# Loading each weight piece as two transfers of 64 partitions, and moving two transposes by one product

## The chip, the cores and the metric

The kernel runs on one NeuronCore of a Trainium2 chip. The metric is the device time of one execution in microseconds. All runs of the kernel before lie between 2293 and 2320 us. A ratio is the mean time of one kernel's runs over the mean of the other's runs of the same rounds on the same chip, so it is not quite the ratio of the medians that stand beside it.

## The reference

Two branches on `x` (2048 tokens of 1024) are mixed by a gate. Branch A is a recurrent attention with memory, in 64 segments of 32 tokens. Each segment needs the 8 memory rows that the segment before produced, so the 64 steps cannot overlap freely. Branch B is a gated feed-forward network.

```python
for s in range(n_seg):                      # 64 segments, one after the other
    xs = x[:, s * seg_len:(s + 1) * seg_len, :].copy()
    h = jnp.concatenate([mem, xs], axis=1)  # 8 + 32 rows
    q = jnp.einsum('btd,dhe->bhte', h, Wq)  # Wq, Wk, Wv: 1024 x 32 heads x 128
    k = jnp.einsum('btd,dhe->bhte', h, Wk)
    v = jnp.einsum('btd,dhe->bhte', h, Wv)
    scores = jnp.einsum('bhqe,bhke->bhqk', q, k) * scale
    # ... mask, softmax -> p ...
    o = jnp.einsum('bhqk,bhke->bhqe', p, v)
    o = jnp.einsum('bhte,hed->btd', o, Wo)
    mem = o[:, :M, :].copy()
    outs.append(o[:, M:, :])
# branch B: gelu(x @ w_gate) * (x @ w_up) @ w_down;  result g * a + (1 - g) * b
```

## The kernel before

The four weight matrices of branch A are cut into 64 pieces of 512 KB (128 partitions by 2048 bf16). The program does not hold all of them on the chip at once. It has 52 slots, and 12 of them are shared by two pieces each: when a product has used one piece, its slot is refilled with the other. So every step fetches 12 pieces, in the order in which slots come free: 2 of Wk, 2 of Wq, 5 of Wv, 3 of Wo. The order of products alternates from step to step, so that each fetch serves two uses.

```python
        PAIRS = {"k": (0, 2), "q": (0, 2), "v": (0, 1, 2, 4, 6), "o": (0, 2, 4)}
        ORDER = (("k", 0), ("q", 0), ("v", 0), ("k", 1), ("q", 1), ("o", 0), ("v", 1), ("o", 1))
        # ... (cut)
        def fetch(n):
            k, t = uses[n][done[n]], slots[n]
            if paired(k):
                lane = f"sl{n}"
            else:
                lane = f"res{nlane[0] % 8}"
                nlane[0] += 1
            op("sp", lambda e: e.dma_start(dst(t, k), src(k)), wr=[t.r()], lane=lane)
        # ... (cut)
        def spent(k):                    # called behind each product
            n = home[k]
            done[n] += 1
            if done[n] < len(uses[n]) and uses[n][done[n]] != k:
                fetch(n)
```

`op` records an instruction and finds its waits from the regions that it reads and writes; a lane is a semaphore, and the program counts a load as 16 on it (in the trace, 16 packets of 4 bytes a piece). SyncE ("sp") issues all these loads in order. A row of a Wk, Wq or Wv piece is 4 KB in one run; a row of a Wo piece is two runs of 2 KB, one for each of its two heads. In the trace they are packets of 4,096 and 2,048 bytes.

In each step, a finished block of eight products is copied by ScalarE from PSUM, the memory that the products write, into `tok`, transposed on TensorE a few products later, and copied on by VectorE. `on(block, half, n, f)` puts `f` ahead of product `n` of a block:

```python
            on("q", 0, 0, lambda: evac(bank_of["k", 0], tok))
            on("q", 0, 5, lambda: trans(kT))
            on("v", 0, 0, lambda: evac(bank_of["q", 0], tok))
            on("v", 0, 4, lambda: trans(qT))
            on("k", 1, 0, lambda: evac(bank_of["v", 0], vA))
            on("k", 1, 0, lambda: scores(0))
            # ... (cut)
            on("q", 1, 4, lambda: trans(kT))
```

## Time and profile before

| | before |
|---|---|
| median of 3 runs | 2307.32 us (2305.66 to 2311.26) |
| profiled span | 2304.5 us |
| end of the first step, of the last but one | 140.9, 1659.9 us |
| mean step of the recurrence (62 intervals) | 24.50 us |
| SyncE queue's work in a step | 17.39 us of all 16 DMA engines |

A step is counted here from one copy of the new memory rows into `hT` to the next. The queue's work is the sum of the times of its packets in the recurrence, divided by 16 engines and by the number of steps; 12 pieces make 1.45 us a piece.

From the page of the kernel before: the span, TensorE's busy time, then three rows of 40 equal slices (granted TensorE clock in tenths, DMA busy share in tenths, GB/s), and SyncE's DMA queue (packets, MB, share of 16 engines' span).

```profile
span 2304.5 us, 80168 instructions
...
PE 2060.9 (89%) x36594; PEld 1099.2 (48%) x36614; DVE 901.2 (39%) x2164; ACT 604.1 (26%) x1280; POOL 616.0 (27%) x1107
...
PEclk9999999999999999999999999999999999999999
DMA  9968788788788787787887887887782802606206
GB/s 358 379 213 305 257 304 294 261 289 309 265 303 302 272 316 271 269 322 265 290 323 248 302 302 256 302 303 266 270 330 90 276 34 80 230 1 208 103 1 237
...
q1 hardware_dynamic: 189536, 513.35, 61.7%
```

TensorE is 89% busy. During the recurrence (slices 3 to 29) the DMA engines are mostly 70 to 90% busy, which is an average over full and empty stretches. The view of windows shows these (busy time of each engine, then granted clock, DMA busy share, GB/s), for three stretches of one step of the kernel before:

```profile
core 0: us, PE busy (x) PEld busy (x) DVE busy (x) ACT busy (x) POOL busy (x), PEclk, DMA share, GB/s
905.00:909.00 4.00, 3.55 (x66) 1.65 (x59) 3.03 (x9) 1.03 (x2) 1.95 (x4) 1.00 1.02 399
912.00:915.00 3.00, 2.50 (x95) 1.82 (x98) 1.82 (x6) 1.26 (x3) 0.07 (x2) 1.00 1.02 379
919.50:922.50 3.00, 2.55 (x61) 1.55 (x57) 0.46 (x3) 0.65 (x3) 1.03 (x3) 1.00 0.09 29
```

Where loads wait in the queue, it moves 380 to 400 GB/s with all engines busy. At the end of the step it is nearly empty, because the next slots come free only when the next step begins. The issues of SyncE in this step (start, duration, x number of loads), from the timeline of the kernel before:

```profile
899.97 1.07 SPq L363 DMA_DIRECT2D sl<-in_A_Wq_dram  x2
902.14 2.25 SPq L363 DMA_DIRECT2D sl<-in_A_Wv_dram  x5
911.96 2.13 SPq L363 DMA_DIRECT2D sl<-in_A_Wo_dram  x3
922.71 0.82 SPq L363 DMA_DIRECT2D sl<-in_A_Wk_dram  x2
```

Five Wv loads are issued in 2.25 us and, by their semaphores, land between 909.97 and 915.63 us, 1.2 to 1.8 us apart. The queue there is limited by transfer (1.2 to 1.8 us a piece) and not by issue (0.45 us a piece). From the page of the kernel before, the chain that ended last, by engine and by line:

```profile
PE 65%; DMA 24%; issue 5%; DVE 3%; ACT 2%; POOL 1%; SPq 0%; ACTq 0%; POOLq 0%; DVEq 0%
PE pb L670 20%; PE pb L929 14%; DMA sl<-in_A_Wq_dram 11%; PE pb L682 9%; PE pb L697 6%; PE pb L966 6%; DMA sl<-in_A_Wo_dram 5%; PE pb L712 3%; PE pb L588 3%; DMA sl<-in_A_Wv_dram 3%; DMA wd<-in_B_w_down_dram 2%; PE pb L609 1%; DMA xr_scr<-x
```

DMA has 24% of it, mostly Wq and Wo pieces. From the same page, the loads of the Wv and Wo pieces (number, KB each, median us from issue to landing), and the group of the transposes (number, busy us, mean ns, idle time of TensorE before them and its releaser):

```profile
sl<-in_A_Wv_dram SPq DMA_DIRECT2D x331, 512.0 KB, 9.9
sl<-in_A_Wo_dram SPq DMA_DIRECT2D x205, 512.0 KB, 5.9
```

```profile
L588 PE MATMUL pb<-ident,tok 128*128 128x128 bf16 x1280 | 128.1, 222 | 13.2 <-ACT tok L576 8.9
```

### The profile page before, as it was taken

Reading aid. Unit: us, or ns where it says so; the run is one execution under the profiler, and the core shown is the slowest. Engines: PE = TensorE matmul, PEld = TensorE weight load, DVE = VectorE, ACT = ScalarE, POOL = GpSimd, SP = SyncE. Lnnn points to the kernel's source line nnn. Section 1 sums busy time; section 2 is a strip of 40 time slices with the busy share of each in tenths; the row PEclk is TensorE's granted clock in tenths of the full one; section 3 lists DMA queues with packets and bytes.
Section 4 is the critical chain, followed back from the end, with each engine's and each line's share of the span. In section 5 each row is a group of like instructions: output and inputs, shape, how many; then the busy total and the mean of one; then the engine's idle time right before and its main releaser. Section 6 shows DMA issues by size and latency. Waiting matters only on the chain.

```text
span 2304.5 us, 80168 instructions
## 1 busy us (share of the span) xinstructions
PE 2060.9 (89%) x36594; PEld 1099.2 (48%) x36614; DVE 901.2 (39%) x2164; ACT 604.1 (26%) x1280; POOL 616.0 (27%) x1107
## 2 busy tenths in 40 slices
PE   2588998899999998898998998998879999999998
PEld 1244555555555555555555455554444444444443
DVE  3134333334334343343343433333335164363452
ACT  1122232222323222232232322222223032131230
POOL 5233333343333433333333333333210000000000
PEclk9999999999999999999999999999999999999999
DMA  9968788788788787787887887887782802606206
GB/s 358 379 213 305 257 304 294 261 289 309 265 303 302 272 316 271 269 322 265 290 323 248 302 302 256 302 303 266 270 330 90 276 34 80 230 1 208 103 1 237
DMA packets 225714, 576.45 MB, mean 250 GB/s; under 512 B 30424, under 2 KB 42584, under 8 KB 225376
## 3 DMA queue, kind: packets, MB, share of 16 engines
q1 hardware_dynamic: 189536, 513.35, 61.7%
q0 software_dynamic: 26624, 44.14, 5.6%
q10 hardware_dynamic: 9216, 13.83, 1.7%
q8 instruction: 287, 4.70, 0.8%
q14 instruction: 51, 0.42, 0.1%
HBM read 539.71 MB, written 31.39 MB: 248 GB/s over the span
## 4 chain that ended last, share of the span: by engine, by line
PE 65%; DMA 24%; issue 5%; DVE 3%; ACT 2%; POOL 1%; SPq 0%; ACTq 0%; POOLq 0%; DVEq 0%
PE pb L670 20%; PE pb L929 14%; DMA sl<-in_A_Wq_dram 11%; PE pb L682 9%; PE pb L697 6%; PE pb L966 6%; DMA sl<-in_A_Wo_dram 5%; PE pb L712 3%; PE pb L588 3%; DMA sl<-in_A_Wv_dram 3%; DMA wd<-in_B_w_down_dram 2%; PE pb L609 1%; DMA xr_scr<-xr 1%; PE pb L641 1%; PE pb L603 1%
## 5 line engine op out<-in xcount | busy, mean ns | idle before, releaser
L670 PE MATMUL pb<-sl,hT 128*32 128x512 bf16 x12288 | 756.8, 383 | 43.2 <-DMA sl<-in_A_Wq_dram 18.4
L670 PEld LDWEIGHTS pb<-sl,hT 128*32 128x32 bf16 x12288 | 331.7, 97 | 327.2 <-DMA sl<-in_A_Wq_dram 38.8
L682 PE MATMUL pb<-sl,oT 128*32 128x256 bf16 x8192 | 281.8, 275 | 56.2 <-issue 46.1
L576 ACT ACTIVATE tok<-pb 128x512 bf16<-128x512 f32 x320 | 191.0, 597 | 458.0 <-PE pb L670 393.0
L682 PEld LDWEIGHTS pb<-sl,oT 128*32 128x32 bf16 x8192 | 213.0, 97 | 98.7 <-issue 54.6
L697 PE MATMUL pb<-sl,hR 128*32 128x512 bf16 x3072 | 215.0, 390 | 19.6 <-DMA sl<-in_A_Wq_dram 7.3
L929 PE MATMUL pb<-xT,wg 128*128 128x512 bf16 x896 | 213.2, 381 | 16.2 <-DVE GT L945 8.4
L655 POOL COPY oRc<-oT 128x128 bf16<-128x128 bf16 x128 | 98.6, 770 | 452.4 <-DVE oT L579 445.4
L929 PE MATMUL pb<-xT,wu 128*128 128x512 bf16 x896 | 211.7, 379 | 0.0
L966 PE MATMUL pb<-wd,GT 128*128 128x512 bf16 x876 | 194.7, 379 | 8.9 <-DMA wd<-in_B_w_down_dram 7.7
L579 DVE CAST oT<-pb 128x160 bf16<-128x160 f32 x256 | 71.2, 320 | 230.4 <-PE pb L646 230.4
L937 ACT ACTIVATE s<-pb 128x512 f32<-128x512 f32 x112 | 66.8, 596 | 326.8 <-PE pb L929 307.3
L929 PEld LDWEIGHTS pb<-xT,wg 128*128 128x128 bf16 x896 | 87.1, 98 | 125.1 <-DVE GT L945 12.8
L576 ACT ACTIVATE vA<-pb 128x512 bf16<-128x512 f32 x128 | 76.4, 597 | 265.9 <-PE pb L670 265.9
L966 PEld LDWEIGHTS pb<-wd,GT 128*128 128x128 bf16 x896 | 86.4, 98 | 117.2 <-DMA wd<-in_B_w_down_dram 15.5
L588 PE MATMUL pb<-ident,tok 128*128 128x128 bf16 x1280 | 128.1, 222 | 13.2 <-ACT tok L576 8.9
L929 PEld LDWEIGHTS pb<-xT,wu 128*128 128x128 bf16 x896 | 87.7, 98 | 105.9 <-issue 0.3
L938 DVE SCALAR_TENSOR_TENSOR tp<-s,pb 128x512 f32<-128x512 f32 x112 | 76.9, 687 | 155.2 <-ACT s L937 155.1
L588 PEld LDWEIGHTS pb<-ident,tok 128*128 128x128 bf16 x1280 | 72.6, 98 | 123.2 <-ACT tok L576 94.3
L579 DVE COPY kT<-pb 128x512 bf16<-128x512 bf16 x128 | 51.9, 405 | 197.9 <-PE pb L588 197.9
L614 DVE TENSOR_REDUCE st<-pb 128x8 f32<-128x320 f32 x128 | 62.9, 492 | 159.6 <-PE pb L609 159.6
L697 PEld LDWEIGHTS pb<-sl,hR 128*32 128x32 bf16 x3072 | 83.3, 98 | 81.5 <-DMA sl<-in_A_Wq_dram 8.4
(76 smaller groups left out, 1929.7 us busy)
## 6 DMA issues: line engine op xcount, KB each, us to landing
sl<-in_A_Wv_dram SPq DMA_DIRECT2D x331, 512.0 KB, 9.9
sl<-in_A_Wo_dram SPq DMA_DIRECT2D x205, 512.0 KB, 5.9
sl<-in_A_Wk_dram SPq DMA_DIRECT2D x142, 512.0 KB, 5.5
sl<-in_A_Wq_dram SPq DMA_DIRECT2D x142, 512.0 KB, 7.4
wd<-in_B_w_down_dram SPq DMA_DIRECT2D x56, 1024.0 KB, 6.4
qk_scr<-stg POOLq DMA_DIRECT2D x64, 128.0 KB, 5.8
qkr<-qk_scr POOLq DMA_DIRECT2D x128, 64.0 KB, 5.4
wg<-in_B_w_gate_dram SPq DMA_DIRECT2D x3, 1792.0 KB, 13.2
```

The lines of the kernel that those rows point to most:

```text
L576: op("act", lambda e: e.activation(o, i, ACTF.Copy), rd=rd, wr=wr)
L579: op("dve", lambda e: e.tensor_copy(o, i), rd=rd, wr=wr)
L588: ins = e.transpose(PBV[TT][:, j * 128:(j + 1) * 128], tok[:, j * 128:(j + 1) * 128], ident[:, :])
L655: op("pool", lambda e: e.tensor_copy(oRc[:, u, :, :].rearrange("p c x -> p x c"), oT[:, :, :, 32:40].rearrange("p g j c -> p (g j) c")), r ...
L670: ins = e.matmul(PB[bk][32 * g:32 * g + 32, :], lhsT=h[:, i, :], rhs=w[:, g * 512:(g + 1) * 512], start=(p % 8 == 0), stop=(p % 8 == 7))
L682: ins = e.matmul(PB[XO][32 * g:32 * g + 32, 0:256], lhsT=oT[:, gp_, 2 * jj + hh, 0:32], rhs=w[:, c:c + 256], start=(r == 0 and p % 8 == 0 ...
L697: ins = e.matmul(PB[b][32 * g:32 * g + 32, :], lhsT=h[:, k[2], :], rhs=w[:, g * 512:(g + 1) * 512], start=(n == 0), stop=(n == 7))
L712: ins = e.matmul(PB[b][32 * g:32 * g + 32, 0:256], lhsT=t[:, :, 2 * i + hh], rhs=w[:, c:c + 256], start=(ends[0] and i == 0 and hh == 0), ...
L929: ins = e.matmul(PB[bk][:, 0:FB], lhsT=w[:, kc, cc:cc + 128], rhs=xT[:, :, :, kc, :].rearrange("p t i c -> p (t i) c"), start=(kc == 0), s ...
L937: op("act", lambda e, hg=hg: e.activation(s1[:, :], hg, ACTF.Square, scale=SQ), rd=[BK(bg)], wr=[s1.r()])
L938: op("dve", lambda e, hg=hg, t=t: e.scalar_tensor_tensor(out=t[:, :], in0=s1[:, :], scalar=1.0, in1=hg, op0=ALU.add, op1=ALU.mult), rd=[BK ...
L966: ins = e.matmul(PB[bank[2 * k + hf]][:, :], lhsT=GT[:, j, tb * 128:(tb + 1) * 128], rhs=w[:, jj, hf * 512:(hf + 1) * 512], start=(j == 0) ...
```

## The change

Two edits. Every weight piece is loaded as two transfers, partitions 0 to 63 and 64 to 127, both on the piece's semaphore, which now counts 32 for a piece. And two of the transposes (q's first and k's second) are put one product later, so that ScalarE's copy ahead of them has more time.

```diff
-    def op(self, eng, fn, rd=(), wr=(), lane=None, after=()):
+    def op(self, eng, fn, rd=(), wr=(), lane=None, after=(), parts=1):
@@
-            ln[1] += 16
+            ln[1] += 16 * parts
@@ fetch
-            op("sp", lambda e: e.dma_start(dst(t, k), src(k)), wr=[t.r()], lane=lane)
+            sem = []
+
+            def f(e):
+                a, b = dst(t, k), src(k)
+                e.dma_start(a[0:64], b[0:64]).then_inc(sem[0].sem, 16)
+                return e.dma_start(a[64:128], b[64:128])
+            sem.append(op("sp", f, wr=[t.r()], lane=lane, parts=2))
@@
-            on("v", 0, 4, lambda: trans(qT))
+            on("v", 0, 5, lambda: trans(qT))
@@
-            on("q", 1, 4, lambda: trans(kT))
+            on("q", 1, 5, lambda: trans(kT))
```

## The prediction

> **What bounds the kernel now.** The page gives a span of 2304.5 us. From about 80 to 1680 us (the view of the weight tiles) runs a recurrence of 64 steps; the timeline shows one from 899.9 to 924.4 us. TensorE is 89% busy, but the chain of waits gives DMA 24% of the span: Wq pieces 11%, Wo 5%, Wv 3%. A step fetches 12 pieces of 512 KB as slots come free. Its five Wv pieces are issued within 2.3 us and land, by their semaphores, 1.2 to 1.8 us apart (909.97 to 915.63 us): there the queue is limited by transfer, not by issue (330 to 440 ns each). It moves about 400 GB/s; in the packet records a 4 KB packet takes 159 ns, 25.8 GB/s on each of 16 engines. The last Wv piece lands at 915.63 us and is used within about 1 us; the last Wo piece lands at 919.47 us, and its block runs from 918.88 to 921.4 us. Then the queue is empty until 923.7 us. So the last pieces have about 1 us of slack in a step.
>
> **What the change does.** (1) 820 loads become 1640. Issue: about 0.35 us more of SyncE per piece, 4 us a step, against 780 + 555 us in which the queue waits for products (its own waits): not critical. Extra semaphore packets: 9 ns per engine and piece. Both halves must land, so no product starts earlier. (2) Each half writes partitions 0 to 63 or 64 to 127 alone. [...] My estimate: a backlogged piece goes from about 1.3 to between 1.5 and 2.4 us. (3) Transposes: in the timeline q's start 0.14 us after its ScalarE copy ends, without a visible hole; PE's idle time before this line is 13.2 us in all, 8.9 by ScalarE. The later copy of q still ends about 0.2 us before the scores. Gain: 0 to 8 us.
>
> **On the critical path.** Of (2), all beyond 1 us a step. At 1.6 us a piece: 12 x 0.3 - 1 = 2.6 us a step, 165 us in all. At 2.4 us: near 7 us a step, 450 us. Without conflicts: 0 to -10 us.
>
> **Prediction.** 2430 us, range 2275 to 2760. Two modes: near 2300 (no conflict), or 2370 to 2780. Faster by over 2%: 0.12; within 2%: 0.33; slower by over 2%: 0.55.
>
> **What would show it.** Right: the median 4 KB packet well above 159 ns, or a tail near 300; Wv pieces over 1.5 us apart; Wv and Wo landings longer than 9.9 and 5.9 us; DMA's share of the chain above 24%; the queue's empty stretch filled. The transposes' idle time falls from 13.2 us, and the scores' waits for q's copy do not grow. Wrong: 159 ns and 1.2 us stay.
>
> **What would make it wrong.** [...] (now a burst's first pieces land about 2 us apart) and the Wq landing of 7.4 us falls, which could gain up to 3%.

The author's estimate starts from 1.3 us, about eight 4 KB packets of 159 ns on each engine in the trace before, and assumes 0.2 to 1.1 us on top, 0.3 in the sum; no load of that trace showed such a slowdown. Measured later, a backlogged Wv piece took 2.15 us. "Conflict" stands for this assumed slowdown. The sum: at 1.6 us a piece it is 12 x 0.3 - 1 = 2.6 us a step, 165 us over the 64 steps, or about 2470 us; the forecast of 2430 us lies between that and the mode near 2300. The median Wq landing, 7.4 us before, stayed at 7.4 (of half pieces).

## The result, and the profile after

| | before | after |
|---|---|---|
| median | 2307.64 us (4 runs) | 2867.26 us (4 runs, 2864.65 to 2871.80) |
| ratio | | 1.2425 (95% interval 1.2401 to 1.2449) |
| profiled span | 2304.5 us | 2870.0 us |
| end of the first step, of the last but one | 140.9, 1659.9 us | 166.5, 2213.8 us |
| mean step | 24.50 us | 33.02 us |
| SyncE queue's work in a step | 17.39 us | 25.75 us |

The time is 24% longer, outside the range. The 565.5 us between the two spans are 25.6 us up to the end of the first step, 62 x 8.52 = 528 us in the steps, and 11.5 us behind them. The queue's work per step grew by 8.36 us, nearly what the step grew by.

The page of the kernel after, the same lines:

```profile
span 2870.0 us, 81008 instructions
...
PE 2252.5 (78%) x36614; PEld 1126.9 (39%) x36614; DVE 905.8 (32%) x2164; ACT 604.1 (21%) x1280; POOL 615.4 (21%) x1107
...
PEclk9898889999899988998899899988878899999999
DMA  9978888888888889888888888888888926070705
GB/s 290 307 175 215 214 211 204 224 220 217 213 201 216 223 211 229 205 207 211 215 223 217 206 206 224 215 214 215 204 202 210 294 100 209 5 245 1 245 4 191
...
q1 hardware_dynamic: 202656, 513.41, 69.1%
```

The same bytes take 69.1% of a span that is a quarter longer, and hardly a slice of the recurrence passes 225 GB/s, where 290 was common. TensorE's busy time grew by 192 us with the same work, because its clock is no longer full: 454.6 us are spent at half clock, against 44.9 before (from the trace's clock records), and there four products of 128x512 start a median of 427 ns after the four before them, against 216 ns at full clock. In the recurrence this is not idle time: in 389 us at half clock TensorE is busy for 342 us. Windows of one step of the kernel after, two of them with a full queue and one at the end of the step:

```profile
core 0: us, PE busy (x) PEld busy (x) DVE busy (x) ACT busy (x) POOL busy (x), PEclk, DMA share, GB/s
1104.00:1111.00 7.00, 6.57 (x181) 4.41 (x177) 3.52 (x10) 1.32 (x4) 2.58 (x5) 0.80 1.03 248
1115.00:1118.00 3.00, 3.00 (x48) 1.03 (x44) 0.08 (x1) 0.68 (x2) 0.00 (x0) 0.50 1.06 244
1120.50:1123.50 3.00, 2.51 (x66) 1.53 (x58) 0.34 (x2) 0.45 (x2) 0.96 (x2) 1.00 0.07 22
```

All engines are busy, as before, but they move 244 to 248 GB/s in place of 380 to 400. The second window is one at half clock. The empty stretch at the end of the step is still there. SyncE's issues from the timeline of the kernel after:

```profile
1122.96 0.49 SPq L367 DMA_DIRECT2D sl<-in_A_Wk_dram  x1
1123.49 0.60 SPq L368 DMA_DIRECT2D sl<-in_A_Wk_dram  x1
...
1132.08 0.60 SPq L368 DMA_DIRECT2D sl<-in_A_Wv_dram  x1
1132.72 0.59 SPq L367 DMA_DIRECT2D sl<-in_A_Wv_dram  x1
```

A load of 64 partitions takes SyncE 0.60 us, more than a whole piece took before (five in 2.25 us). The chain of the kernel after, and its loads:

```profile
PE 49%; DMA 39%; SPq 4%; issue 4%; DVE 2%; ACT 1%; POOL 0%; ACTq 0%; POOLq 0%
PE pb L676 14%; DMA sl<-in_A_Wq_dram 13%; PE pb L935 12%; DMA sl<-in_A_Wo_dram 11%; DMA sl<-in_A_Wv_dram 9%; PE pb L688 6%; PE pb L972 5%; PE pb L703 5%; SPq L367 3%; PE pb L718 2%; PE pb L594 2%; SPq L368 2%; DMA wd<-in_B_w_down_dram 2%; D
```

```profile
sl<-in_A_Wv_dram SPq DMA_DIRECT2D x662, 256.0 KB, 11.3
sl<-in_A_Wo_dram SPq DMA_DIRECT2D x410, 256.0 KB, 9.4
```

The landing times here are of half pieces, and two loads that share a semaphore are paired with their landings only roughly. The group of the transposes is the same within 0.2 us of idle time:

```profile
L594 PE MATMUL pb<-ident,tok 128*128 128x128 bf16 x1280 | 132.7, 229 | 13.0 <-ACT tok L582 6.1
```

The records of single DMA packets show what changed. A packet here is one run of a row, of 4,096 or 2,048 bytes. This table is worked out from them, for the 4 KB packets of SyncE's queue in the recurrence (experiments included):

```
                       5%   median   mean   95%  ns
before                159     159     178   276
after                 159     267     265   325
even/odd (E4)         159     159     180   293
source spread (E9)    159     271     270   331
dest. spread (E10)    159     159     180   278
```

### The profile page after: what moved, and what is told of

Its sections match the earlier page's. It is cut to its first block, busy times and chain, and to the rows that moved or that the text cites. A ratio compares the mean times of both kernels' runs of the same rounds, so it can differ in the third digit from the quotient of the medians.

```text
span 2870.0 us, 81008 instructions
## 1 busy us (share of the span) xinstructions
PE 2252.5 (78%) x36614; PEld 1126.9 (39%) x36614; DVE 905.8 (32%) x2164; ACT 604.1 (21%) x1280; POOL 615.4 (21%) x1107
## 3 DMA queue, kind: packets, MB, share of 16 engines
q1 hardware_dynamic: 202656, 513.41, 69.1%
## 4 chain that ended last, share of the span: by engine, by line
PE 49%; DMA 39%; SPq 4%; issue 4%; DVE 2%; ACT 1%; POOL 0%; ACTq 0%; POOLq 0%
PE pb L676 14%; DMA sl<-in_A_Wq_dram 13%; PE pb L935 12%; DMA sl<-in_A_Wo_dram 11%; DMA sl<-in_A_Wv_dram 9%; PE pb L688 6%; PE pb L972 5%; PE pb L703 5%; SPq L367 3%; PE pb L718 2%; PE pb L594 2%; SPq L368 2%; DMA wd<-in_B_w_down_dram 2%; DMA xr_scr<-xr 2%; PE pb L615 1%
## 5 line engine op out<-in xcount | busy, mean ns | idle before, releaser
L676 PE MATMUL pb<-sl,hT 128*32 128x512 bf16 x12288 | 839.8, 401 | 325.3 <-DMA sl<-in_A_Wq_dram 127.5
L676 PEld LDWEIGHTS pb<-sl,hT 128*32 128x32 bf16 x12288 | 338.0, 99 | 689.3 <-DMA sl<-in_A_Wq_dram 163.5
L688 PE MATMUL pb<-sl,oT 128*32 128x256 bf16 x8192 | 313.5, 293 | 131.9 <-issue 88.9
L688 PEld LDWEIGHTS pb<-sl,oT 128*32 128x32 bf16 x8192 | 222.8, 103 | 197.5 <-issue 102.5
L703 PE MATMUL pb<-sl,hR 128*32 128x512 bf16 x3072 | 269.4, 473 | 29.4 <-DMA sl<-in_A_Wq_dram 16.2
## 6 DMA issues: line engine op xcount, KB each, us to landing
sl<-in_A_Wv_dram SPq DMA_DIRECT2D x662, 256.0 KB, 11.3
```

Source lines behind the costliest of these rows:

```text
L676: ins = e.matmul(PB[bk][32 * g:32 * g + 32, :], lhsT=h[:, i, :], rhs=w[:, g * 512:(g + 1) * 512], start=(p % 8 == 0), stop=(p % 8 == 7))
L688: ins = e.matmul(PB[XO][32 * g:32 * g + 32, 0:256], lhsT=oT[:, gp_, 2 * jj + hh, 0:32], rhs=w[:, c:c + 256], start=(r == 0 and p % 8 == 0 ...
L703: ins = e.matmul(PB[b][32 * g:32 * g + 32, :], lhsT=h[:, k[2], :], rhs=w[:, g * 512:(g + 1) * 512], start=(n == 0), stop=(n == 7))
```

## The experiments

Theory P, which the prediction carried: the set of partitions that a load writes sets its rate, and a load that writes only 0 to 63, or only 64 to 127, is slower. Before the result this was an assumption. The rivals: the later transposes (T); the number of loads, with their issue and semaphores (N); the DRAM rows that a load reads together (H); and, for the excess over the range, the lost clock (C).

### E1 and E2: the two edits apart

E1 is the change without its last two diff hunks; E2 is those two hunks alone. All later runs but E8 leave the transposes where they were, as E1 does. Most of the diffs below are shown against the change.

> The load split alone, transposes where they were. Theory P [...]: all of the slowdown is here, 2850 to 2880 us, 4 KB packets at a median near 266 ns. Rival T (the later transposes delay the scores and take a part): clearly under 2850 us.

> The two transposes alone, loads whole. Theory P, and my recorded estimate of 0 to 8 us gained: 2298 to 2309 us, ratio 0.996 to 1.001, 4 KB packets at 159 ns. Rival T: above 2330 us.

Measured: E1 2872.29 us (4 runs), ratio 1.2460 (1.2418 to 1.2502). E2 2308.62 us (6 runs), ratio 1.0023 (0.9987 to 1.0059). The load split alone is the whole slowdown, and T falls. The transposes moved nothing: in E2's page their idle time is 12.6 us against 13.2.

### E3: two loads per piece over all 128 partitions

```diff
-                e.dma_start(a[0:64], b[0:64]).then_inc(sem[0].sem, 16)
-                return e.dma_start(a[64:128], b[64:128])
+                if k[0] == "o":
+                    e.dma_start(a[:, 0:1], b[:, 0:1]).then_inc(sem[0].sem, 16)
+                    return e.dma_start(a[:, 1:2], b[:, 1:2])
+                e.dma_start(a[:, 0:1024], b[:, 0:1024]).then_inc(sem[0].sem, 16)
+                return e.dma_start(a[:, 1024:2048], b[:, 1024:2048])
```

> The same 1640 loads of 256 KB, two per piece on one semaphore, but each over all 128 partitions and half of the row (one head of two for Wo). Theory P: near the kernel before, 2300 to 2370 us; the row of 4 KB becomes two of 2 KB (2 x 84 against 159 ns, 6% more transfer, so some 12 x 0.08 = 1 us a step at most). Rival N (the number of loads, their issue on SyncE at 0.6 us each, or the second semaphore packet costs it): as slow as the changed kernel, 2800 us or more.

Measured: 2340.97 us (4 runs), ratio 1.0170 (1.0133 to 1.0206); its steps take 25.03 us. The number of loads and of semaphore packets is that of the change, and so is the size of a load, so these are worth no more than about 2% of the 24. The issue of a load is shorter here than in the change (0.44 against 0.60 us); E4 has it in full. The queue's work rose by 0.47 us a step (17.86 against 17.39), which is the order of the 2 KB packets' extra cost that the expectation named. How much of the 1.7% is packets and how much is the number of loads was not separated.

### E4: two loads of 64 partitions, even and odd

```diff
-                e.dma_start(a[0:64], b[0:64]).then_inc(sem[0].sem, 16)
-                return e.dma_start(a[64:128], b[64:128])
+                e.dma_start(a[0:128:2], b[0:128:2]).then_inc(sem[0].sem, 16)
+                return e.dma_start(a[1:128:2], b[1:128:2])
```

> Two loads of 64 partitions, even ones and odd ones[...]. [...] near the kernel before, under 2400 us. [...] If 64-partition loads are slow for a reason of the DRAM rows or of the issue, also 2700 or more.

Measured: 2364.70 us (4 runs), ratio 1.0261 (1.0230 to 1.0291). This is theory P's case, under 2400 us. So 64 partitions in a load are not slow in themselves. Windows of E4, with a full queue:

```profile
core 0: us, PE busy (x) PEld busy (x) DVE busy (x) ACT busy (x) POOL busy (x), PEclk, DMA share, GB/s
916.00:920.00 4.00, 2.72 (x60) 1.08 (x54) 1.50 (x5) 1.02 (x3) 0.00 (x0) 1.00 1.02 406
```

It moves 406 GB/s and its 4 KB packets are at 159 ns again. The case of 2700 us or more, for a reason of the DRAM rows or of the issue, did not come. SyncE needs 598 ns (median) for a load of 64 partitions in E4, 441 ns for one of 128 partitions of the same 256 KB in E3, and 432 ns for a whole piece in the kernel before. E4 issues 24 loads a step, so this may be the rest of its 2.6%: SyncE (SPq) has 2% of the chain on its page, against 0% before. No run isolates it.

### E9 and E10: the two sides of the transfer apart

E4 changed both the partitions written and the DRAM rows read. These two kernels change one each; they put weight rows into the wrong partitions.

```diff
 E9
-                e.dma_start(a[0:64], b[0:64]).then_inc(sem[0].sem, 16)
-                return e.dma_start(a[64:128], b[64:128])
+                e.dma_start(a[0:64], b[0:128:2]).then_inc(sem[0].sem, 16)
+                return e.dma_start(a[64:128], b[1:128:2])
 E10
+                e.dma_start(a[0:128:2], b[0:64]).then_inc(sem[0].sem, 16)
+                return e.dma_start(a[1:128:2], b[64:128])
```

> Wrong results on purpose: the two loads write partitions 0 to 63 and 64 to 127 as in the change, but read the even and the odd rows of the weight, as the even/odd run does. Theory P (the SBUF side decides): as slow as the split alone, 2840 to 2890 us, 4 KB packets near 267 ns. Rival H (which DRAM rows a load reads together decides): as fast as the even/odd run, 2350 to 2380 us, packets at 159 ns.

> Wrong results on purpose, the other way round: the loads read rows 0 to 63 and 64 to 127 as in the change, and write the even and the odd partitions. Theory P: 2350 to 2380 us, packets at 159 ns. Rival H: 2840 to 2890 us.

Measured: E9 2887.67 us (4 runs), ratio 1.2509 (1.2459 to 1.2559); E10 2359.60 us (4 runs), ratio 1.0238 (1.0185 to 1.0291). Windows over most of the recurrence, E9 first, then E10:

```profile
core 0: us, PE busy (x) PEld busy (x) DVE busy (x) ACT busy (x) POOL busy (x), PEclk, DMA share, GB/s
200.00:2150.00 1950.00, 1497.80 (x30932) 769.68 (x30932) 552.67 (x1575) 418.27 (x953) 530.46 (x983) 0.91 0.88 212
```

```profile
core 0: us, PE busy (x) PEld busy (x) DVE busy (x) ACT busy (x) POOL busy (x), PEclk, DMA share, GB/s
200.00:1650.00 1450.00, 1305.16 (x30125) 724.88 (x30121) 535.68 (x1535) 406.57 (x927) 516.77 (x954) 0.99 0.80 278
```

E9 moves 212 GB/s with the DMA engines 88% busy; E10 moves 278 with 80%. The set of partitions written decides and the DRAM rows do not: H falls. (The comparison with the reference does not see this branch's weights well, so "correct" says little about the loads in any of these runs.)

### E5, E6, E7: the split in some of the pieces only

The whole load stays for the others, for example in E5:

```diff
+                if k[0] not in "v":
+                    return e.dma_start(a, b)
                 e.dma_start(a[0:64], b[0:64]).then_inc(sem[0].sem, 16)
                 return e.dma_start(a[64:128], b[64:128])
-            sem.append(op("sp", f, wr=[t.r()], lane=lane, parts=2))
+            sem.append(op("sp", f, wr=[t.r()], lane=lane, parts=2 if k[0] in "v" else 1))
```

> Only the Wv pieces (5 of 12 in a step) are loaded as lower and upper halves. In the traces a piece takes 1.45 us of all 16 engines whole and 2.15 us as halves, 0.70 us more; all 12 gave 8.5 us a step. Theory A (the queue's service time adds straight into the step, no slack): 5 x 0.70 = 3.5 us a step, 220 us, 2525 us. Theory S (about 1 us of slack a step, and room where the queue is empty): 2.5 us a step or less, 2465 us or less. If the step were set by one late piece alone, its own share decides and the three runs of this kind would not add up to 560 us.

> Only the Wo pieces (3 of 12) as halves. A: 3 x 0.70 = 2.1 us a step, 132 us, 2438 us. S: 1.1 us a step or less, 2375 us or less.

> Only the Wk and Wq pieces (4 of 12) as halves. A: 4 x 0.70 = 2.8 us a step, 176 us, 2482 us. S: 1.8 us a step or less, 2420 us or less. A and S are told apart best by the sum of the three gains against the 560 us of all: near 530 to 560 for A, 360 or less for S.

Measured (step and queue work from each profile, as growth over the kernel before):

```
            median us  ratio (95%)                step    queue's work   per split piece
E5 Wv (5)    2703.10   1.1737 (1.1703, 1.1772)    +6.07      +5.53            1.11
E6 Wo (3)    2465.03   1.0700 (1.0682, 1.0718)    +2.37      +2.10            0.70
E7 Wk,Wq (4) 2550.45   1.1067 (1.1027, 1.1108)    +3.54      +2.83            0.71
after (12)   2867.26   1.2425 (1.2401, 1.2449)    +8.52      +8.36            0.70
```

Both A and S missed in numbers. In all four kernels the step grew by at least as much as the queue's work (1.02 to 1.25 times), so no net slack of 1 us a step shows, and S is refuted. (The time at half clock grew as well, by 1.5 to 4.9 us a step in E5 to E7, so the growth need not be transfer alone.) But the cost of a split piece is not the fixed 0.70 us that A used: for Wv alone it is 1.11, and the three slowdowns add up to 806 us where all pieces together give 560. E5's windows show the cost within one step: whole Wk and Wq pieces, then Wv halves, then whole Wo pieces.

```profile
core 0: us, PE busy (x) PEld busy (x) DVE busy (x) ACT busy (x) POOL busy (x), PEclk, DMA share, GB/s
1043.00:1044.00 1.00, 1.00 (x24) 0.65 (x20) 0.50 (x2) 0.75 (x2) 0.69 (x2) 1.00 1.04 418
1050.00:1055.00 5.00, 3.71 (x128) 2.79 (x128) 3.26 (x9) 0.44 (x1) 1.48 (x3) 1.00 1.03 236
1057.00:1058.00 1.00, 0.00 (x0) 0.00 (x0) 0.00 (x0) 0.00 (x0) 0.00 (x0) 1.00 1.04 375
```

The rate falls from 418 to 236 GB/s with the first halves and returns with the whole pieces, the engines being busy throughout. At these rates a piece of 524,288 bytes takes 1.25 and 2.22 us, 0.97 more. The five Wv pieces sit in this full part of the queue. The first pieces of a burst do not: in the kernel before, the records give the first pieces only 90 to 280 GB/s for the two to three microseconds after the empty stretch, so there is less to take away.

The packets show where the rest comes from. The records do not name the piece of a packet, but if the 4 KB packets are given to the pieces in order of issue (their number, 78,720, fits), their mean times in the recurrence are these, with those of the 2 KB packets of Wo:

```
               Wk    Wq    Wv    Wo (2 KB)   mean ns
before        227   168   162    93
after         244   273   269   133
E5 Wv split   224   168   286   104
E6 Wo split   221   169   168   133
E7 Wk,Wq      243   271   181    96
```

In the change a Wk piece (128 packets, in the mean 8 for each of 16 engines) costs 0.14 us more by these means, a Wq piece 0.84, a Wv piece 0.86 and a Wo piece (16 for each) 0.63; 0.70 is only their mean. In a partial split, whole pieces behind split ones became slower too: Wv in E7 (0.74 us a step), Wo in E5 (0.49), Wv in E6 (0.21). With the slower Wv packets of E5 itself (286 in place of 269 ns, 0.68 us a step) this is all of the 2.1 us by which the three growths of the queue's work exceed 8.36. The remaining excess of the three slowdowns, some 1.4 us a step, lies outside the queue's work and was not followed. Why a whole piece is slow behind a split one stays open: the records do not name the engine of a packet.

### E8: keeping TensorE's clock up

```diff
+        WARM = {("k", 30): 4, ("q", 37): 4, ("q", 38): 12, ("v", 53): 6, ("v", 54): 8}
+            n_warm = WARM.get((k[0], p), 0) if 0 < s else 0
+            if n_warm:
 ... (cut: n_warm matmuls 128x256 of hT by ident into the unused bank F1, ahead of product p)
```

In the trace of the change, TensorE had been idle for at least 1.1 of the 3 us ahead of each of the 88 stretches at half clock in the recurrence, and for 2.1 us in the mean; over all stretches of 3 us the mean is 0.7. An added product takes about 0.11 us at full clock by an estimate: in the kernel before, the 128x512 products of branch B (L966) start a median of 216 ns apart, and an added one has half their columns.

> The changed kernel with idle products (34 of 128x256 a step into an unused bank, about 3.6 us at full clock) just ahead of the loads that it waits for longest, so that TensorE stays busy and its clock is not cut; the trace of the changed kernel has 6.2 us a step at half clock. Theory C (the clock lost in those waits is a large part of the excess over my range): 2780 us or less. Theory D (transfer decides, the half clock falls into waits): 2830 to 2900 us, with the time at half clock clearly down.

Measured: 2889.14 us (4 runs), ratio to the kernel before 1.2540 (1.2518 to 1.2562), 0.8% above the change. From the windows of E8 over most of the recurrence:

```profile
core 0: us, PE busy (x) PEld busy (x) DVE busy (x) ACT busy (x) POOL busy (x), PEclk, DMA share, GB/s
200.00:2150.00 1950.00, 1669.38 (x32807) 915.78 (x32807) 552.99 (x1565) 417.84 (x950) 530.05 (x979) 0.95 0.87 212
```

The time at half clock fell from 6.2 to 3.1 us a step and the granted clock of the stretch rose from 0.90 to 0.95, yet the step did not shorten (33.21 us). So C in its strong form falls. The added products may cost time where a load has landed already, so a small gain may be hidden. In the changed kernel itself, the 17 steps of 60 with at most 0.5 us at half clock in their last 8 us take 32.63 us and the other 43 take 33.19 us, so 0.4 us a step (25 us in all) is what this comparison would give the clock. It does not separate cause from effect, since a longer wait both lengthens a step and can come before a lower clock.

The landings say more. In the changed kernel the last product of a step starts within 0.1 us of the landing of the step's last Wo piece in 38 of 62 steps, and 0.26 us after it in the mean. With these landings, and by an estimate from the 0.26, a TensorE at full clock could have ended the steps some 0.3 us earlier at most. What the clock costs by freeing slots later was not isolated.

## Why the prediction was wrong

- **Direction, and the side that decides: right**, though the prediction gave "slower by over 2%" only 0.55. The split slows the transfer because of the partitions each load writes. E1 puts all of it on the split (1.2460), E3 excludes the number of loads (1.0170), E4 shows that 64 partitions can be loaded at full rate (406 GB/s), and E9 and E10 show that the written side decides (1.2509 and 1.0238). Why a lower or an upper half is slow, the runs do not show.
- **Size: wrong, and this is the step that failed.** "My estimate: a backlogged piece goes from about 1.3 to between 1.5 and 2.4 us": the band was right, but the sum took 1.6 from it, 0.3 us more a piece. Measured, a backlogged Wv piece goes from 1.30 to 2.15 us by its packets (8 x 162, then 8 x 269 ns), and from 1.25 to 2.22 us by the rates in one step of E5. Over all 12 pieces, start of bursts included, it is from 1.45 to 2.15 us, 0.70 a piece. The 1.6 us, which would be a mean of 200 ns a packet, was the author's estimate alone, and too low: the Wv packets' mean is 269. Only 8% of the 4 KB packets of the recurrence kept within 150 to 165 ns, against 83% before.
- **The top of the range was also computed badly.** "At 2.4 us: near 7 us a step, 450 us." By the prediction's own formula it is 12 x (2.4 - 1.3) - 1 = 12.2 us a step, which would be some 780 us. So the range ended at 2760 while the stated service time reached far beyond it. With the measured 2.15 us the formula gives 12 x 0.85 - 1 = 9.2 us a step, some 590 us, near the measured 560. That nearness is partly luck: two of the 12 pieces (Wk) cost only 0.14 us more each, and the slack was not what the formula took off.
- **The slack of "about 1 us" could not be subtracted.** The step grew by 8.52 us where the queue's work grew by 8.36, and each partial split (E5 to E7) lengthened the step by no less than the queue's added work. Something of that kind was there: in the kernel before, the last Wo piece lands 0.89 us in the mean ahead of its product, after the change 0.26. But this is a mean; in 21 of 62 steps it was at most 0.1 us already before, and other pieces of the step, Wq's second above all, were already waited for. What took the 0.6 us back was not isolated.
- **Left out:** the fill before the first step (25.6 us) and the stretch behind the recurrence (11.5 us).
- **"the queue's empty stretch filled": wrong.** It stayed (22 GB/s in its window), because the next loads wait for the next step's products, not for the queue. Over the recurrence, the queue lands under 40 GB/s for 4.7 us a step before and 4.4 us after.
- **Issue: wrong in size, and in part on the path.** The prediction gave a piece 0.35 us more of SyncE. It is 1.2 us in place of 0.43. SyncE has 4% of the chain after (SPq), against 0% before, where the prediction called it not critical. E4, with the same issue, loses 2.6% in all, so there it is worth no more than that.
- **Transposes: right in size.** 0 to 8 us of gain were expected; E2 shows 1.0023 with an interval that holds 1 and reaches down to 0.9987. Their idle time, which was to fall, stayed (13.2, then 13.0 us); it says little, since it is anywhere from 9.4 us (E4) to 20.8 (E1) in kernels whose transposes were not moved.
- **The other signs named for the split came**: packets at a median of 267 ns, Wv pieces that land 2.0 to 2.7 us apart (1105.78 to 1114.77 us, one step), DMA at 39% of the chain, and Wv and Wo landings up from 9.9 and 5.9 us to 11.3 and 9.4 us.
- **Not foreseen:** the half clock that comes with the waits. TensorE's busy time rose by 192 us with it; E8 and the landings of the last Wo piece find little of this on the path.

## What to carry to other kernels

When a load like these is cut in two, cut it so that each part still covers the same spread of partitions: by columns (1.7% of the time here), or by even and odd partitions (2.6%), and not into a lower and an upper half (24.6%). When a queue is full for most of a step and its loads are waited for, put the added transfer time straight into the step, times the number of loads, and look for slack only where an experiment shows it. When a range has an upper case, compute it with the same formula as the central one.
